# A fused sliding-window attention and MLP-mixer kernel: the last output block in three pieces, and all order lists searched anew

## The chip, the cores and the metric

The kernel runs on one core of a Trainium2 chip. The metric is the device time of one execution in microseconds (us); lower is better. Each version is run several times beside runs of the kernel before on the same chip. Every run here is fast, that is undisturbed; the clock that was granted to PE was 0.997 to 1.0 of full speed. A ratio is the mean time of one kernel's fast runs over that of the other's fast runs of the same rounds, so it isn't quite the ratio of the medians that are quoted beside it.

Besides the time there is one profiled execution of each kernel. Its span (from the first to the last instruction) is about 1.8 us shorter than the time, and positions inside it are read to 0.01 us.

## The reference, cut to what matters

```python
# attention: batch 8, heads 8, sequence 576, head size 64, window 128, ALiBi bias
scores = scale * q @ k.T + slopes * -(i - j)       # kept where 0 <= i - j < 128
attn = softmax(scores)
x = concat_heads(attn @ v)                         # (8, 576, 512)
# mixer
h = relu(x.T @ w_tok1) @ w_tok2                    # mixing over tokens, 576 -> 256 -> 576
u = x + h.T
out = u + relu(u @ w_ch1) @ w_ch2                  # mixing over channels, 512 -> 1536 -> 512
```

## The kernel before

Every piece of work has a short name, and five lists give the order in which the pieces are emitted; each engine then runs its own instructions in that order. A prime (') means the next batch. So while batch b is in the channel mixing, pieces of batches b+1 to b+3 are woven in.

- S: scores of a key block; A, AT: transposes of q and k on the tensor engine (PE), of strips and of the token tails; P, p: attention times v; K, k and U, u: the two steps of token mixing; UT: the second step for the last 64 tokens; X, x: transposes of u.
- C: a 128-wide strip of the first channel product (12 a batch, 4 matmuls of 512 columns each); D: an output block (12 such matmuls, in three parts D?0, D?1, D?2); T, E: the same for the token tails.
- q, l, qt, v, G, H: loads, of q, k, their tails, v, and the two channel weights. M: exponentials that make the mask. W: matmuls that only keep PE busy.

```python
def M():                         # three PSUM banks take turns, in the order of emission
    t = psM[mrot[0] % 3]
    mrot[0] += 1
    return t
...
def half(w):                     # only in the very last block, b == 7 and c == 3
    t = M()
    for ht in range(NHT):        # 12 matmuls of 256 columns
        nc.tensor.matmul(t[:, 0:256], lhsT=r2[b % 2][:, ht, c * P:(c + 1) * P],
                         rhs=WC2[:, ht, w:w + 256], start=(ht == 0), stop=(ht == NHT - 1))
    o = ob[orot[0] % len(ob)]
    orot[0] += 1
    nc.vector.tensor_tensor(out=o[:, 0:256], in0=t[:, 0:256], in1=ub[b % 2][:, c, w:w + 256], op=ALU.add)
    nc.sync.dma_start(out=out[b, c * P:(c + 1) * P, w:w + 256], in_=o[:, 0:256])
...
emit(PROLOGUE); emit(FIRST)      # batch 0 and the first scores of batch 1
emit(SECOND, 1)
for b in range(2, B - 1):
    emit(PERIOD, b)              # five times the same list
emit(LAST, B - 1)
```

A piece that asks for a bank may not start until the engine that empties that bank's last content has done so.

The softmax here doesn't subtract the row's maximum and nothing guards it: scores larger than these inputs give would overflow.

## Time and profile before

| | before |
|---|---|
| time, median | 288.33 us |
| span of the profiled execution | 286.7 us |
| PE busy | 278.9 us (97%) |
| VectorE, ScalarE, GpSimd busy | 57%, 41%, 35% |
| stops of PE of over 0.2 us after the first 11 us; the last is at 54 us | about 3.1 us |
| from the last matmul's end to the end of the span | 3.47 us |

A "stop" here is time by which a matmul starts later than its forerunner's length allows: 0.216 us after one of 512 columns, 0.109 after 256, 0.056 after 128. The profile's own idle time starts only where the earlier matmul's record ends, which is 0.16 us later, so it shows less, or nothing for a short stop. The chain of work that ended last, by engine, is nearly all PE:

```profile
PE 93%; ACT 3%; issue 1%; DVE 1%; DVEq 0%
```

### The profile page before, as it was taken

The numbers are of one execution on the slowest core, as the hardware profiler recorded it, in microseconds if no ns is written. First come the engines' busy times: TensorE is split into PE (matmuls) and PEld (weight loads), VectorE is DVE, ScalarE is ACT, GpSimd is POOL, SyncE is SP. The second block draws the span as 40 slices with busy tenths as digits, with TensorE's granted clock in tenths as the row PEclk, the third lists the DMA queues.
The fourth block names the chain that finished last, engine by engine and source line by source line (L and its number), as shares of the span: only waits on it lengthen the run. The fifth ranks groups of instructions, "written<-read, shape, count | busy, mean of one in ns | idle before, by whom it ended". The sixth has DMA issues, their size and how long they took to land.

```text
span 286.7 us, 6107 instructions
## 1 busy us (share of the span) xinstructions
PE 278.9 (97%) x2514; PEld 155.4 (54%) x2535; DVE 164.8 (57%) x329; ACT 118.6 (41%) x182; POOL 101.4 (35%) x132
## 2 busy tenths in 40 slices
PE   8999999999999999999999999999999999999995
PEld 3577546464565556545664456545664456455452
DVE  5359766537668376745556666745556666523222
ACT  3898941148515443326542343326542343104300
POOL 8997443099199029501870008900000000000000
PEclk9999999999999999999999999999999999999999
DMA  9999999799999989987999279999304310052032
GB/s 196 167 199 191 207 177 135 171 161 146 167 191 199 143 210 110 155 164 187 107 156 160 110 122 155 149 182 168 84 2 110 112 37 2 37 146 57 0 92 93
DMA packets 150267, 38.38 MB, mean 134 GB/s; under 512 B 137440, under 2 KB 145760, under 8 KB 150240
## 3 DMA queue, kind: packets, MB, share of 16 engines
q0 software_dynamic: 103152, 17.41, 84.0%
q1 hardware_dynamic: 46544, 20.06, 29.4%
q10 hardware_dynamic: 544, 0.52, 0.5%
q8 instruction: 20, 0.33, 0.5%
q14 instruction: 7, 0.06, 0.1%
HBM read 35.85 MB, written 9.44 MB: 158 GB/s over the span
## 4 chain that ended last, share of the span: by engine, by line
PE 93%; ACT 3%; issue 1%; DVE 1%; DVEq 0%
PE psM L548 29%; PE psM L607 28%; PE psM L506 4%; PE psM L481 4%; PE psS L356 4%; PE psT L565 4%; PE psM L629 4%; PE psS L420 2%; PE psS L416 2%; PE psT L750 2%; PE psS L448 1%; PE psM L588 1%; PE psS L360 1%; PE psM L234 1%; PE psM L490 1%
## 5 line engine op out<-in xcount | busy, mean ns | idle before, releaser
L548 PE MATMUL psM<-utb,WC 128*128 128x512 bf16 x384 | 90.9, 379 | 0.0
L607 PE MATMUL psM<-WC,r 128*128 128x512 bf16 x353 | 84.2, 379 | 0.7
L370 ACT ACTIVATE pe<-psS 128x1024 bf16<-128x1024 f32 x56 | 54.6, 1024 | 38.0 <-PE psS L356 34.4
L607 PEld LDWEIGHTS <-r 128*128 128x128 bf16 x372 | 34.5, 98 | 40.1 <-issue 3.1
L548 PEld LDWEIGHTS <-WC 128*128 128x128 bf16 x384 | 34.6, 98 | 36.3 <-issue 1.5
L376 DVE TENSOR_TENSOR pb<-pe,masks 128x1024 bf16<-128x1024 bf16 x42 | 29.0, 691 | 26.3 <-ACT pe L370 26.2
L554 ACT ACTIVATE r<-psM 128x512 bf16<-128x512 f32 x48 | 28.5, 599 | 35.5 <-PE psM L548 35.4
L190 POOL DMA_DIRECT2D qn<-in_q_dram x24 | 21.1, 907 | 59.2 <-DMA qT<-qn 58.7
L551 DVE TENSOR_SCALAR r<-psM 128x512 bf16<-128x512 f32 x48 | 32.6, 686 | 15.8 <-PE psM L548 15.6
L612 DVE TENSOR_TENSOR ob<-psM,ub 128x512 f32<-128x512 f32 x31 | 21.0, 687 | 27.4 <-PE psM L607 19.5
L190 POOL DMA_DIRECT2D vp<-in_v_dram x32 | 28.7, 928 | 0.7 <-PE psM L607 0.3
L190 POOL DMA_DIRECT2D kn<-in_k_dram x24 | 21.2, 911 | 18.1 <-DMA kT<-kn 11.8
L430 DVE TENSOR_TENSOR xb<-psS,rt 128x512 bf16<-128x512 f32 x28 | 19.4, 691 | 1.0
L508 DVE TENSOR_TENSOR ub<-psM,xb 128x512 bf16<-128x512 f32 x28 | 17.5, 681 | 2.6 <-PE psM L506 2.6
L568 ACT ACTIVATE r2t<-psT 128x512 bf16<-128x512 f32 x12 | 7.2, 600 | 24.8 <-PE psT L565 24.8
L420 PEld LDWEIGHTS <-pb 128*128 128x128 bf16 x224 | 13.5, 97 | 4.3 <-issue 1.0
L420 PE MATMUL psS<-vp,pb 128*128 128x65 bf16 x224 | 15.6, 193 | 0.0
L506 PE MATMUL psM<-r,W 128*128 128x512 bf16 x56 | 14.5, 379 | 0.5 <-DVE ob L612 0.5
L499 ACT ACTIVATE r<-psM 128x512 bf16<-128x512 f32 x7 | 4.2, 596 | 25.0 <-PE psM L490 25.0
L356 PE MATMUL psS<-qT,kT 64*128 64x256 bf16 x168 | 13.2, 271 | 0.7
L481 PE MATMUL psM<-xb,W 128*128 128x256 bf16 x112 | 13.4, 273 | 0.0
L565 PEld LDWEIGHTS <-WC 128*128 128x128 bf16 x192 | 11.6, 98 | 2.2
(134 smaller groups left out, 302.7 us busy)
## 6 DMA issues: line engine op xcount, KB each, us to landing
out_dram<-ob SPq DMA_DIRECT2D x31, 256.0 KB, 2.1
vp<-in_v_dram POOLq DMA_DIRECT2D x32, 128.0 KB, 5.4
kn<-in_k_dram POOLq DMA_DIRECT2D x24, 128.0 KB, 6.0
qn<-in_q_dram POOLq DMA_DIRECT2D x24, 128.0 KB, 6.1
WC<-in_moe_w_ch_dram POOLq DMA_DIRECT2D x3, 512.0 KB, 8.8
WC<-in_moe_w_ch_dram POOLq DMA_DIRECT2D x2, 768.0 KB, 14.2
out_dram<-ob SPq DMA_DIRECT2D x10, 128.0 KB, 2.3
qs<-in_q_dram POOLq DMA_DIRECT2D x3, 256.0 KB, 6.2
```

What stands on the lines that cost most here:

```text
L190: nc.gpsimd.dma_start(out=dst, in_=src[b, :, c * P:(c + 1) * P, :].rearrange("h s d -> s h d"))
L356: nc.tensor.matmul(s[h][:, a * 256:(a + 1) * 256], lhsT=kT[i][r, kb, hp, :], rhs=qT[i][r, kb:kb + 2, hp, :], start=True, stop=True)
L370: nc.scalar.activation(out=e[:, h, :], in_=s[n][:, None, :] if split else t2[:, :, :], func=ACT.Exp, scale=scale)
L376: nc.vector.tensor_tensor(out=p[:, :].rearrange("p (h x) -> p h x", h=2), in0=e[:, :, :], in1=masks[:, j].rearrange("p h g a x -> p h (g a ...
L420: nc.tensor.matmul(ov, lhsT=prob(b, qb, h, 0), rhs=vt[:, qb, h, 0:D + 1], start=first, stop=(hh == 3))
L481: nc.tensor.matmul(st["t"][h][:, dh * 256:(dh + 1) * 256], lhsT=W1[:, c, dh * P:(dh + 1) * P], rhs=by_half(xb[b % 2][:, c, :])[:, h], star ...
L506: nc.tensor.matmul(t[:, :], lhsT=W2[:, j, c * P:(c + 1) * P], rhs=r1[b % 2][:, j, :], start=(j == 0), stop=(j == 1))
L548: nc.tensor.matmul(t[:, :], lhsT=WC1[:, cb, ht * P:(ht + 1) * P], rhs=utb[b % 2][:, :, cb, :], start=(cb == 0), stop=(cb == NCB - 1))
L551: nc.vector.tensor_scalar(out=r2[b % 2][:, ht, :], in0=t[:, :], scalar1=0.0, scalar2=None, op0=ALU.max)
L554: nc.scalar.activation(out=r2[b % 2][:, ht, :], in_=t[:, :], func=ACT.Relu)
L565: nc.tensor.matmul(psT[:, j * P:(j + 1) * P], lhsT=WC1[:, cb, ht * P:(ht + 1) * P], rhs=utt[pi2][:, cb, :, :], start=(j == 0 and cb == 0), ...
L607: nc.tensor.matmul(t[:, :], lhsT=r2[b % 2][:, ht, c * P:(c + 1) * P], rhs=WC2[:, ht, :], start=(ht == 0), stop=(ht == NHT - 1))
```

## The change

The intent is to shorten the way from the last matmul to the end of the kernel (a smaller last addition and a smaller last store), and to search all order lists again, with the first loads of q named ahead of those of k.

```diff
-        def half(w):
+        def piece(w, n):
             t = M()
...
         if b == B - 1 and c == NC - 1:
-            return [lambda: half(0)] + [lambda: None] * (parts - 2) + [lambda: half(256)]
+            return [lambda: piece(0, 256), lambda: piece(256, P), lambda: piece(384, P)]
...
-U_ACT = (2,)
+U_ACT = (1, 2)          # strips of batch 0 whose residual PE adds, by identity matmuls
-X_DVE = (0, 2)          # which copies of X go to VectorE, the others to ScalarE
+X_DVE = (0, 3)
-K_DVE = (0,)            # which relu of K goes to VectorE
+K_DVE = (1,)
...
-SPLIT = (1, 2, 3, 4, 5) # scores of batch 0 whose exponential is done in two parts
+SPLIT = (0, 1, 2, 3, 4, 5)
...
-x_DVE = (0, 1, 2)       # as X_DVE and K_DVE, for the first batch
-k_DVE = (2, 3)
+x_DVE = (0, 2)
+k_DVE = (1,)
-AK_DVE = (1, 3, 6)      # which copies of transposes go to VectorE, which to ScalarE
-AQ_ACT = (0, 2, 4, 5, 6)
+AK_DVE = (3, 6, 7)
+AQ_ACT = (0, 1, 4, 5, 6, 7)
 PERIOD (its first third):
-Zq'' Lq''' C0 C7 T0 C6 C3 S31' S30' C4 P2' Zk'' Lk''' Y C10 C8 C9 P1' C2 T1 C1 P4' C11 P3' C5
+T1 C0 C6 C3 S30' S31' C2 Zq'' C7 C10 Zk'' T2 P2' C8 P3' C9 P1' C4 C5 T0 Lq''' C1 C11 P4' Y Lk'''
 LAST (its end):
-... D10 D30 D11 D20 D12 D31 D21 D22 D32
+... D10 D11 D12 D20 D21 D30 D22 D31 D32
 (PROLOGUE, FIRST and SECOND are all new too; cut)
```

More of the change, by code (lines that the diff above doesn't have):

```diff
@@ L19 @@
 U_DMA = (3, 4, 5, 6, 7)
-U_ACT = (2,)
-X_DVE = (0, 2)
-K_DVE = (0,)
+U_ACT = (1, 2)
+X_DVE = (0, 3)
+K_DVE = (1,)
 PROLOGUE = """
-l0 FC q0 J l1 O W4 q1 v4 q23 ck0 I l23 W3 W1 W2 B cq0 A0 ck1 v3 cq1 qt v0 s1 A1 S00 v2 t1 S20 W3
-ek v1 A3 A2 LW q01' AT l01' ex e2 S11 S30 l23' S21 M1 p0 LC S01 p1 k0 q23' e1 S31 u0 M0 M2 k1 G0
-p3 A1' qt' p2 A0' m0
+q0 q1 W3 J l0 l1 v4 FC l23 I ck0 W2 W4 W1 B v3 q23 cq0 O qt A0 ek ck1 s1 cq1 A1 S00 t1 v2 S20 W3
+v0 v1 LW A2 A3 AT q01' e2 S11 S30 l01' S21 ex M1 LC p0 l23' M2 p1 S01 k0 S31 u0 M0 m0 q23' G0 k1
@@ L27 @@
+p3 M3 A1' p2 qt' A0' v4'
 """
 FIRST = """
-A2' v3' G1 u1 k3 S10' A3' v4' G2 M3 H0 k2 H1 m1 v0' x0 AT' S00' v2' S20' u3 v1' W2 Lk'' UT u2
-Lq'' x3 Zq'' Zk'' x1 Lk''' x2 v0''' S30' E0 C5 v0'' S31' S01' v3'' C8 C9 C3 C11 C1 v1'' Lq'''
-S21' S11' C10 v2'' C7 C4 P4' C0 E2 C2 P0' C6 P3' v4'' v2''' D00 D01 P1' v4''' P2' D02 K0' K1'
-D10 D11 U1' D12 Zq''' X1' U3' U2' D20 U0' D21 D30 UT' Zk''' D22 S00'' D31 X0' D32 E1 T0' X2'
+G2 u1 G1 A3' S10' A2' k3 H1 AT' v2' e1 k2 v3' H0 x0 m1 v0' S00' S20' u3 W2 UT v1' Lq'' E0 Lk''
@@ L33 @@
+u2 x1 x3 Zq'' Zk'' Lk''' x2 v0'' S30' C2 C3 v0''' S01' S31' C11 C5 C1 Lq''' v1'' S21' v2'' S11'
+C0 C10 C7 v3'' C4 P4' v4''' E2 C8 P0' C9 v2''' C6 v4'' P3' P1' D00 P2' D01 D02 K0' K1' D10 D11
+U1' D12 U3' U2' X1' E1 D20 Zq''' Zk''' U0' D21 D30 D22 UT' S00'' D31 D32 X0' T0'
 """
 SECOND = """
-X3 Lq''' Lk''' S31' S30' T2 C10 v3''' S20' C5 S01' S11' v0''' C1 C8 C4 v1'' C11 C2 P0' C7 C9
-v3'' S10' S21' C3 C6 T1 C0 P2' v2''' v1''' P1' D00 D01 P3' P4' D02 K0' K1' S01'' S10'' D10 D11
-D12 v4''' U0' UT' U1' U3' U2' X0' S11'' S20'' D20 X3' D21 S00'' S21'' D22 E0 E1 X2' D30 E2 D31
@@ L38 @@
-X1' D32 P0''
+X2 X3 S30' S20' T1 Lq''' C1 C0 S11' Lk''' S01' T2 C5 v1'' S31' C3 P0' C10 C2 v3'' v3''' C4 S10'
+v0''' S21' C6 C11 C8 C7 v1''' v4''' C9 P2' P1' D00 P3' D01 D02 P4' K0' K1' S20'' S01'' D10 D11
+v2''' D12 U0' UT' U2' U3' X0' S11'' S10'' U1' D20 X3' D21 S21'' S00'' D22 E0 E1 X2' E2 D30 X1'
+D31 D32 P0''
 """
 PERIOD = """
-Zq'' Lq''' C0 C7 T0 C6 C3 S31' S30' C4 P2' Zk'' Lk''' Y C10 C8 C9 P1' C2 T1 C1 P4' C11 P3' C5
-K0' v4''' T2 K1' S01'' S00'' D00 v3''' v0''' D01 D02 U0' v1''' U3' UT' U2' U1' X1' P0'' v2'''
@@ L43 @@
-D20 D21 D10 X2' S10'' S11'' D11 X0' D22 D12 D30 D31 D32 S21'' S20'' X3' E0 E1 E2
+T1 C0 C6 C3 S30' S31' C2 Zq'' C7 C10 Zk'' T2 P2' C8 P3' C9 P1' C4 C5 T0 Lq''' C1 C11 P4' Y Lk'''
+K0' v0''' K1' S01'' v3''' S00'' v1''' D00 D01 D02 v2''' U1' v4''' U3' UT' U2' P0'' U0' D20 D21
+X2' X0' S10'' S11'' D10 D30 D11 D12 D22 D31 S20'' X1' S21'' D32 E0 E1 X3' E2
 """
 LAST = """
-T1 C0 C1 T0 Y C11 C2 C10 T2 C7 C3 C8 C6 C5 C4 C9 D00 E0 D01 D02 E1 E2 D10 D30 D11 D20 D12 D31
-D21 D22 D32
+C5 T0 Y C6 C0 C8 C10 C7 C1 C2 T1 C3 C11 T2 C9 C4 D00 E0 D01 D02 E1 E2 D10 D11 D12 D20 D21 D30
@@ L48 @@
+D22 D31 D32
 """
@@ L583, in ch2 @@
         st = {}
-        def half(w):
+        def piece(w, n):
             t = M()
             for ht in range(NHT):
-                nc.tensor.matmul(t[:, 0:256], lhsT=r2[b % 2][:, ht, c * P:(c + 1) * P],
-                                 rhs=WC2[:, ht, w:w + 256], start=(ht == 0), stop=(ht == NHT - 1))
+                nc.tensor.matmul(t[:, 0:n], lhsT=r2[b % 2][:, ht, c * P:(c + 1) * P],
+                                 rhs=WC2[:, ht, w:w + n], start=(ht == 0), stop=(ht == NHT - 1))
             o = ob[orot[0] % len(ob)]
             orot[0] += 1
-            nc.vector.tensor_tensor(out=o[:, 0:256], in0=t[:, 0:256], in1=ub[b % 2][:, c, w:w + 256],
+            nc.vector.tensor_tensor(out=o[:, 0:n], in0=t[:, 0:n], in1=ub[b % 2][:, c, w:w + n],
                                     op=ALU.add)
-            nc.sync.dma_start(out=out[b, c * P:(c + 1) * P, w:w + 256], in_=o[:, 0:256])
+            nc.sync.dma_start(out=out[b, c * P:(c + 1) * P, w:w + n], in_=o[:, 0:n])
         if b == B - 1 and c == NC - 1:
-            return [lambda: half(0)] + [lambda: None] * (parts - 2) + [lambda: half(256)]
+            return [lambda: piece(0, 256), lambda: piece(256, P), lambda: piece(384, P)]
         def part(pi):
```

## The prediction

> **What bounds the kernel now.** I read the page's first two parts first: which engine is full, and in which part of the span.
>
> ```profile
> PE 278.9 (97%) x2514; PEld 155.4 (54%) x2535; DVE 164.8 (57%) x329; ACT 118.6 (41%) x182; POOL 101.4 (35%) x132
> PE   8999999999999999999999999999999999999995
> PEclk9999999999999999999999999999999999999999
> ```
>
> PE is full in every slice but the first and the last, at full clock; no other engine passes 57%. Busy time alone can deceive, so I took the start-to-start times of neighbouring matmuls from the trace: a 512-column matmul follows its forerunner after 0.216 us through the whole channel-mixing work, so PE isn't only busy there but at its pace. The lines of the windows view divide the span into start, body and end:
>
> ```profile
> 0.00:14.00 14.00, 12.37 (x113) 5.87 (x113) 6.30 (x26) 8.22 (x15) 13.22 (x24) 1.00 1.46 181
> 14.00:34.00 20.00, 19.39 (x352) 14.62 (x351) 14.48 (x40) 17.74 (x38) 15.40 (x22) 1.00 1.43 198
> 130.00:260.00 130.00, 129.19 (x1101) 70.92 (x1111) 76.88 (x142) 48.57 (x68) 25.14 (x30) 1.00 0.87 112
> 281.70:286.70 5.00, 1.50 (x13) 1.07 (x11) 1.11 (x2) 0.00 (x0) 0.00 (x0) 1.00 0.36 131
> ```
>
> The reader is to see that 0.8 of 130 us is idle in the periodic body, that ACT is busy 17.74 of 20 us in the second stretch (the only place where another engine nearly binds), and that PE works only 1.5 of the last 5 us. What PE ever waited for, from the waits of PE alone, is short:
>
> ```profile
> PE psM L506 <- DVE ob L612: 0.5, 1, 0.5
> PE psM L234 <- DVE qT L239: 0.4, 1, 0.4
> PE psM L739 <- DVE ub L732: 0.2, 1, 0.2
> PE psM L259 <- DVE kT L239: 0.2, 1, 0.2
> ```
>
> Smaller stops hide in the 0.22 us that a matmul record lasts. Counting start-to-start excess, I find 0.53 and 0.35 us at 11.8 and 12.5 us (transposes of the first batch, waiting for a bank), 0.25 at 16.5 (scores S01, a bank), four of 0.24 from 23.0 to 27.1 (transposes of the second batch, waiting for ScalarE's copies), 0.39 at 30.1 and 0.63 at 53.6: 3.1 us in all, the whole stock from which an order alone can win. At the end, the timeline shows the path that sets the time:
>
> ```profile
> 281.73 1.47 PE L588 MATMUL psM<-WC,r 128*128 128x256 bf16 x12
> 281.93 0.69 DVE L612 TENSOR_TENSOR ob<-psM,ub 128x512 f32<-128x512 f32 x1 [1.03 <-PE psM L607]
> 283.24 0.42 DVE L592 TENSOR_TENSOR ob<-psM,ub 128x256 f32<-128x256 f32 x1 [0.62 <-PE psM L588]
> 283.69 0.33 SPq L594 DMA_DIRECT2D out_dram<-ob  x1
> ```
>
> The last matmul ends at 283.20; addition, store and landing (285.38 in the trace) follow one another, then 1.29 us of closing semaphores.
>
> **What the Trainium skill says.** "Perfetto Trace Analysis", section Identifying the Most-Contended Engine, warns that matmul busy share is no measure of nearness to the limit; here it agrees with the pace, since the pace is 0.216 us. "TensorE: Matmul & The Clock Gate", section Back-to-back issue gap, gives N/2.4 + 2.5 ns warm: 216, 109 and 56 ns for 512, 256 and 128 columns. The trace has 216, 109 and 56 to 57 (each with its own weight load), so the alternative of 81 ns for N=128 that the same section gives for a load-and-multiply stream isn't seen here. "VectorE: DVE Perf Modes", section on the TRN2 errata, gives (N+151)/0.96 ns for an fp32 tensor_tensor: 691, 424, 291; the rows have 687, 424 and 291 (the 128-column one from L690). "DMA: Bandwidth & Descriptors", section Anatomy of one DMA — SWDGE, has about 2.0 us of fixed cost; the last 128 KB store, on the other path, lands 1.70 us after its issue, so size hardly counts.
>
> **The change, part by part.**
> Final pieces. The last half of 256 columns becomes two of 128: 24 matmuls at 56 ns for 12 at 109. The last start moves from 281.73 + 11 x 0.109 = 282.93 to 281.73 + 23 x 0.056 = 283.01, and its record is 0.22 instead of 0.27 us long: end 283.23, 0.03 later. The addition shrinks from 0.424 to 0.291: the store starts at about 283.58 instead of 283.69. The earlier piece's addition is queued behind that of the 512-wide block, which ends at 282.62, so it is done by 282.95 and not in the way. Store: 64 instead of 128 KB, at most 0.1 quicker. Gain 0.1 to 0.2, say 0.12 us.
> U_ACT. The second strip of the first batch now adds its residual by four identity matmuls: 4 x 0.056 = 0.23 us more on PE, for certain; it frees 0.69 us of VectorE and puts 0.6 on ScalarE.
> Orders. A count of PE's instruction list shows only these 12 + 4 extra matmuls; changes between 64-row and 128-row work, at 0.09 us each, are 78 in both. So all else is about stops:
> - 11.1 to 13.6 us: the third strip's copies now go one to VectorE, one to ScalarE; before, both of the first pair stood in VectorE's queue. The two stops should fall from 0.87 to about 0.4, but VectorE then runs three copies of 0.69 from 11.60 to about 13.6, which the next scores need. They began at 13.69; gain 0.1.
> - 16.5: p1 now stands ahead of S01, so the bank has time: 0.25 gained. But M2 was moved up: four mask exponentials at 0.33 us instead of two ahead of S01's on ScalarE, which pushes the relu of k0 from 18.9 to about 19.2, ending 19.6, while u0, which needs it, would come at 19.3. Given back: net 0.
> - 23 to 27: A0' and A2' no longer stand side by side, u1 lies between. With ScalarE's copies at 0.48 us pitch, the three stops go; one of some 0.45 at AT', behind the 1.02 us exponential of S10', may stay. Gain 0.45.
> - 30.1: x1 stands before x3, whose copy was late; x2 still waits for the end of u2's copy. Gain 0.1.
> - 53.6: U3' stood one 0.23 us transpose after D12 and waited for D12's 0.69 us addition; now U3' takes a free bank for 0.43 us and U2' waits. Gain 0.2.
> - First v loads of batch 1: before, v0' landed at 40.89 and the first P0' began at 42.99. One more 128 KB load now stands ahead of it (pitch 0.87 us), so 41.8; P0' is placed about 1.1 us earlier, at 41.9. The slack is spent; I charge 0.15.
> - q ahead of k at the very start: q is issued by ACT and k by SP, at 0.73 and 0.74 us, in both kernels. No gain.
> - Body: loads and transposes keep their order on SP; on GpSimd only the v loads change places. 0.
>
> Sum: -0.12 + 0.23 - 0.1 - 0 - 0.45 - 0.1 - 0.2 + 0.15 = about -0.6. Discounted for steps that give back, -0.45 on 288.33: **287.9 us**.
>
> **The rivals.**
> 1. The stops are all removed. A search over the orders could reach what my block-by-block reading gives up: 3.1 us of stock less 0.23, plus 0.12 at the end, at best -3.0, in practice perhaps -1.5: 286.8. For it: the lists were changed everywhere. Against: the start is a chain of copies on ScalarE (17.74 of 20 us busy), which no order on PE shortens.
> 2. A new wait in the periodic body. It is repeated five times, so a stop of 0.3 us there costs 1.5: 289.8. For it: C blocks alternate between two evicting engines and new neighbours could put three on one; P3' and P1' stand nearer one another. Against: in the new order no more than three evictions of 0.69 stand on VectorE against 0.86 us of matmuls each, and K1' still has K0' (1.75 us) between it and P4'.
> 3. A late load: if v0' slips further than 0.9, P0' stops for it; another 0.5 would give 288.4.
> 4. The split is hidden: if the closing semaphores wait for some other store, the tail keeps its 3.5 us; 288.0.
>
> **Range and chances.** The three runs of before already spread by 0.6 us. Against that, my terms are each 0.1 to 0.5 and uncertain to half their size. 8 in 10: **286.9 to 288.7**. Faster by over 2% would need 5.8 us, nearly twice the stock of stops: 0.005. Slower by over 2% would need over 1 us in each period: 0.01. Within 2%: 0.985.
>
> **What would show it right or wrong.** PE busy should stay at 278 to 279.5 us and the spacing in the body at 0.216. Right: no stops at 23 to 24 us, the one near 53.6 down to about 0.4, a last 128-column addition of 0.29 us, its store issued about 0.35 us after the last matmul, and from that matmul's end to the span's end about 3.3 us instead of 3.47. Wrong: a PE wait on vp from a DMA near 42 us above 0.3 (rival 3), a wait on ScalarE or VectorE that returns every 32 us (rival 2), or first-batch relu waits near 19.3 above 0.5. If the first D block (44.59 before) starts before 43.9 with P1' now in front of it, the start won more than I give it (rival 1).

## The result, and the profile after

The changed kernel takes **287.95 us** (median of 5 runs, 287.49 to 288.23) against 288.33 us; the ratio is 0.9992, with a 95% interval of 0.9974 to 1.0009. By the times alone that is no difference. The two profiled spans are 286.67 and 286.18 us.

The page of the changed kernel, busy time of the engines, PE by slices, and the chain that ended last:

```profile
PE 277.5 (97%) x2532; PEld 155.8 (54%) x2551; DVE 165.4 (58%) x328; ACT 119.8 (42%) x185; POOL 101.5 (35%) x132
...
PE   8999999999999999999999999999999999999995
...
PE 83%; DMA 8%; POOL 6%; issue 1%; DVE 1%; POOLq 0%
```

PE looks as before. But the chain now runs through loads (DMA 8%) and GpSimd, which issues them, where it was PE from the start: at one point PE's progress has come to hang on a load. The windows view of the changed kernel, in the stretches shown of before (the last one is again the last 5 us; columns are the stretch, its length, then busy time and instructions of PE, weight loads, VectorE, ScalarE, GpSimd, then granted clock, DMA share and GB/s):

```profile
0.00:14.00 14.00, 12.29 (x121) 6.23 (x122) 7.32 (x29) 7.92 (x16) 13.16 (x25) 1.00 1.45 180
14.00:34.00 20.00, 19.27 (x354) 14.62 (x351) 13.29 (x35) 18.66 (x41) 14.62 (x20) 1.00 1.38 200
130.00:260.00 130.00, 128.83 (x1099) 70.61 (x1105) 77.76 (x142) 48.20 (x67) 25.16 (x30) 1.00 0.80 113
281.20:286.20 5.00, 1.72 (x26) 1.36 (x23) 1.25 (x3) 0.00 (x0) 0.00 (x0) 0.98 0.31 105
```

In the second stretch VectorE has 1.2 us less work and ScalarE 0.9 us more; it is now busy for 18.66 of 20 us. The waits of PE in the changed kernel (six of nine lines):

```profile
PE psM L607 <- issue: 1.8, 11, 0.2
PE psS L420 <- DMA vp<-in_v_dram: 0.5, 1, 0.5
PE psM L506 <- DVE ob L612: 0.3, 1, 0.3
PE psM L722 <- ACT r L713: 0.3, 1, 0.3
PE psM L259 <- ACT qT L239: 0.3, 1, 0.3
PE psM L234 <- DVE qT L239: 0.3, 1, 0.3
```

The first line is no wait: at these eleven places a matmul's record is missing. This also lowers the busy time of PE, 277.5 us; e1, whose PE does the same work and whose trace has all 2551 records, shows 279.2. Of the waits shown of before, those for VectorE's ub and kT have gone; three are new: for a load of v (L420, the block P0'), for a relu on ScalarE (L722, u0), and for a copy on ScalarE (L259, the tail transposes AT'). The end, from the timeline:

```profile
281.25 1.77 PE L588 MATMUL psM<-WC,r 128*128 128x128 bf16 x24
281.45 0.69 DVE L612 TENSOR_TENSOR ob<-psM,ub 128x512 f32<-128x512 f32 x1 [0.44 <-PE psM L607]
282.12 0.29 DVE L592 TENSOR_TENSOR ob<-psM,ub 128x128 f32<-128x128 f32 x1
282.60 1.12 SPq L594 DMA_DIRECT2D out_dram<-ob  x2
283.07 0.29 DVE L592 TENSOR_TENSOR ob<-psM,ub 128x128 f32<-128x128 f32 x1 [0.65 <-PE psM L588]
```

The 24 matmuls of the two small pieces take 1.77 us; at 56 ns each they should take 23 x 0.056 + 0.22 = 1.51. In the trace 0.275 us is lost between the first and the second matmul of the last piece, until 282.20, just after the 512-wide addition (281.45 + 0.69 = 282.14) is through.

Cutting both spans at the same places of the work gives a balance (positions in us from the span's start):

| stretch | before | after | difference |
|---|---|---|---|
| start, up to the scores S00 of the third batch (L356) | 59.48 | 59.57 | +0.09 |
| first channel-mixing matmul of batch 1's period to that of batch 7's | 61.77 to 257.01 = 195.24 | 61.86 to 256.54 = 194.68 | -0.56 |
| from there to the last matmul's start | 25.92 | 26.27 | +0.35 |
| last matmul's start to the end of the span | 3.75 | 3.37 | -0.37 |
| sum (spans: -0.49) | | | -0.49 |

So the start, where nearly all stops were, gained nothing; the body gained; and the two parts of the end nearly cancel.

### The profile page after: what moved, and what is told of

Its sections match the earlier page's. It is cut to its first block, busy times and chain, and to the rows that moved or that the text cites. A ratio compares the mean times of both kernels' runs of the same rounds, so it can differ in the third digit from the quotient of the medians.

```text
span 286.2 us, 6156 instructions
## 1 busy us (share of the span) xinstructions
PE 277.5 (97%) x2532; PEld 155.8 (54%) x2551; DVE 165.4 (58%) x328; ACT 119.8 (42%) x185; POOL 101.5 (35%) x132
## 3 DMA queue, kind: packets, MB, share of 16 engines
q1 hardware_dynamic: 46688, 20.06, 30.1%
## 4 chain that ended last, share of the span: by engine, by line
PE 83%; DMA 8%; POOL 6%; issue 1%; DVE 1%; POOLq 0%
PE psM L607 28%; PE psM L548 26%; DMA vp<-in_v_dram 5%; PE psM L481 4%; PE psM L506 4%; PE psT L565 4%; PE psM L629 4%; PE psS L356 3%; DMA WC<-in_moe_w_ch_dram 3%; PE psS L420 2%; PE psS L416 2%; POOL vp L190 2%; PE psS L448 1%; PE psM L490 1%; POOL qs L200 1%
## 5 line engine op out<-in xcount | busy, mean ns | idle before, releaser
L548 PE MATMUL psM<-utb,WC 128*128 128x512 bf16 x384 | 89.7, 379 | 0.0
L607 PE MATMUL psM<-WC,r 128*128 128x512 bf16 x353 | 83.3, 379 | 2.2 <-issue 1.8
L370 ACT ACTIVATE pe<-psS 128x1024 bf16<-128x1024 f32 x56 | 54.5, 1023 | 33.2 <-PE psS L356 30.1
L420 PE MATMUL psS<-vp,pb 128*128 128x65 bf16 x224 | 15.6, 193 | 0.5 <-DMA vp<-in_v_dram 0.5
L420 PEld LDWEIGHTS <-pb 128*128 128x128 bf16 x224 | 13.5, 97 | 4.4 <-DMA vp<-in_v_dram 1.0
L506 PE MATMUL psM<-r,W 128*128 128x512 bf16 x56 | 15.5, 379 | 0.3 <-DVE ob L612 0.3
L356 PE MATMUL psS<-qT,kT 64*128 64x256 bf16 x168 | 13.1, 271 | 0.0
```

The lines of the kernel that those rows point to most:

```text
L356: nc.tensor.matmul(s[h][:, a * 256:(a + 1) * 256], lhsT=kT[i][r, kb, hp, :], rhs=qT[i][r, kb:kb + 2, hp, :], start=True, stop=True)
L370: nc.scalar.activation(out=e[:, h, :], in_=s[n][:, None, :] if split else t2[:, :, :], func=ACT.Exp, scale=scale)
L420: nc.tensor.matmul(ov, lhsT=prob(b, qb, h, 0), rhs=vt[:, qb, h, 0:D + 1], start=first, stop=(hh == 3))
L506: nc.tensor.matmul(t[:, :], lhsT=W2[:, j, c * P:(c + 1) * P], rhs=r1[b % 2][:, j, :], start=(j == 0), stop=(j == 1))
L548: nc.tensor.matmul(t[:, :], lhsT=WC1[:, cb, ht * P:(ht + 1) * P], rhs=utb[b % 2][:, :, cb, :], start=(cb == 0), stop=(cb == NCB - 1))
L607: nc.tensor.matmul(t[:, :], lhsT=r2[b % 2][:, ht, c * P:(c + 1) * P], rhs=WC2[:, ht, :], start=(ht == 0), stop=(ht == NHT - 1))
```

## The experiments

"On" names the kernel that an experiment starts from. The ratio is to the kernel before, with its 95% interval.

| label | on | time, median | ratio | span |
|---|---|---|---|---|
| e1_v0_early | changed | 287.65 | 0.9975 (0.9960 to 0.9990) | 286.1 |
| e2_spare_bank | changed | 287.89 | 0.9984 (0.9966 to 1.0002) | 285.8 |
| e3_two_halves | changed | 287.74 | 0.9980 (0.9965 to 0.9995) | 285.7 |
| e4_masks_back | changed | 288.05 | 0.9993 (0.9976 to 1.0010) | 286.0 |
| e5_tail_load | changed | 288.02 | 0.9990 (0.9975 to 1.0005) | 286.5 |
| e6_both_loads | changed | 286.93 | 0.9960 (0.9943 to 0.9976) | 285.2 |
| e7_all_four | changed | 286.60 | 0.9945 (0.9930 to 0.9959) | 285.3 |
| e8_period_only | before | 287.69 | 0.9984 (0.9969 to 0.9999) | 285.9 |
| e9_q_first | e7 | 286.74 | 0.9942 (0.9927 to 0.9957) | 285.0 |
| e10_one_strip | e7 | 286.80 | 0.9945 (0.9929 to 0.9962) | 285.0 |
| e11_tail_between | e7 | 286.10 | 0.9922 (0.9907 to 0.9937) | 284.4 |
| e12_best | e7 | 286.09 | 0.9939 (0.9926 to 0.9951) | 284.3 |

All twelve gave the reference's result.

### e1_v0_early: one load of v earlier

```diff
 FIRST
-... H1 AT' v2' e1 k2 v3' H0 x0 m1 v0' S00' ...
+... H1 AT' v0' e1 k2 v3' H0 x0 m1 v2' S00' ...
```

> The changed kernel with two loads of the second batch exchanged (v0 ahead of the second half of the output weights, v2 behind it). Theory: the 0.64 us stop of PE before the first P0' near 41.6 us is the late landing of v0' (42.37 us) and nothing else; v0' now lands near 36.4, the stop falls to under 0.1, and everything after it starts 0.5 to 0.65 us earlier: span 285.6 instead of 286.2. Rival: the DMA queue is the limit at this place, so the wait moves to P3' or P1' (which read v2' and v1', landing near 42.4 and 43.2), and the span stays within 0.15 us of 286.2.

In the changed kernel the stop before P0' looks like this (timeline of PE, changed kernel):

```profile
40.92 1.02 PE L548 MATMUL psM<-utb,WC 128*128 128x512 bf16 x4
42.42 0.42 PE L420 MATMUL psS<-vp,pb 128*128 128x65 bf16 x8 [0.48 <-DMA vp<-in_v_dram]
```

With v0' moved, it landed at 36.96 instead of 42.37 us and this stop was gone. Yet the span was 286.13, as before the edit, so the theory's number failed. The rival's place (P3', P1') showed no stop either. The trace has the time elsewhere, and earlier: at the tail transposes (timeline of PE, e1):

```profile
25.46 0.22 PE L706 MATMUL psM<-xt,W1t 128*128 128x128 bf16 x1
26.90 0.38 PE L259 MATMUL psM<-ident,qkt 128*128 128x128 bf16 x4 [1.22 <-DMA qkt<-in_k_dram]
```

Here PE waits for another load, the q and k tails of batch 1. They landed at 26.76 us in this execution, and at 26.18 in the profiled one of the changed kernel, where the same place had cost 0.49 us. This made the next question: is it the loads as a whole that pace the start?

### e2_spare_bank: another bank for the last piece

```diff
         def piece(w, n):
-            t = M()
+            t = psT if w == 384 else M()
```

> The changed kernel with the very last 128-column piece in the PSUM bank that the tail work has left free. Theory: the 0.275 us stop inside the last piece (its first matmul against its second, 281.87 to 282.20 us) is the wait for the addition of the 512-wide block in the same rotating bank; with the free bank it is under 0.05, the last matmul starts 0.25 to 0.3 us earlier relative to the first matmul of that block, and the span shrinks by 0.15 to 0.3. Rival: VectorE's queue is the limit at the end (0.69 + 0.29 + 0.29 us of additions), so the last addition starts at the same place after the 512-wide block's end as now and the span keeps its length.

The theory held. From the first matmul after the periods (256.36) to the last matmul's start took 25.99 us instead of 26.27, 0.27 less. The span fell by 0.39 us, more than expected; 0.21 of this lies in the end (see e3), the rest in the start. End of e2, timeline:

```profile
281.07 0.83 PE L588 MATMUL psM<-WC,r 128*128 128x128 bf16 x12
281.27 0.69 DVE L612 TENSOR_TENSOR ob<-psM,ub 128x512 f32<-128x512 f32 x1 [0.44 <-PE psM L607]
281.74 0.83 PE L588 MATMUL psT<-WC,r 128*128 128x128 bf16 x12
```

The last piece now starts while VectorE still adds the 512-wide block. In the rotation of three, that block's bank is exactly the one that the last piece was given: block D2, piece D30, piece D31, and D32 is back at D2's bank.

### e3_two_halves: the pieces undone, the orders kept

```diff
-            return [lambda: piece(0, 256), lambda: piece(256, P), lambda: piece(384, P)]
+            return [lambda: piece(0, 256), lambda: None, lambda: piece(256, 256)]
```

> The changed kernel with the last block in two halves of 256 again, all orders as changed. Theory from the two traces: from the first matmul of the last half to the last matmul's start 1.20 us instead of 1.56 (with the 0.275 us stop), then 0.27 + 0.42 + 1.7 us to the landing instead of 0.22 + 0.29 + 1.6: the pieces are worth nearly nothing, this one is 0.0 to 0.15 us longer in span. Rival (the change's intent): the shorter last addition and store are a real gain, and this kernel is 0.3 us or more longer.

From the first matmul after the periods (256.08) to the end of the span it took 29.64 us; in the changed kernel 29.64, in e2 29.43. The three pieces as written are thus worth nothing, and 0.21 us once their bank is free. The span as a whole was 0.46 us shorter, where 0.0 to 0.15 longer was expected; all of that lies before the end, in the start. The times (287.74 against 287.95) are too coarse for this.

### e4_masks_back: mask exponentials behind u0 again

```diff
 PROLOGUE
-... p0 l23' M2 p1 S01 k0 S31 u0 M0 m0 ... p3 M3 A1' ...
+... p0 l23' p1 S01 k0 S31 u0 M0 m0 M2 ... p3 A1' ...
 FIRST
-... k3 H1 AT' v2' ...
+... k3 H1 AT' M3 v2' ...
```

> The changed kernel with the mask exponentials M2 behind M0 again (M3 pushed behind the tail transposes of the second batch). Theory: the 0.50 us stop of PE before u0 near 19.0 us is ScalarE's queue (four mask exponentials ahead of the exponentials of S01 and the relu of k0); with two of them there, that stop falls under 0.15 us. ScalarE still has the same sum of work up to 25 us, so part comes back at the transposes of the second batch: first channel-mixing matmul at 31.0 to 31.3 instead of 31.37. Rival: the start is bound by the sum of ScalarE's work, and the first channel-mixing matmul stays at 31.4 or later, the stop before u0 being replaced one for one by stops at 21 to 27 us.

The stop before u0 vanished: from the first matmul of k0 to that of u0 took 1.51 us instead of 1.91. But the first channel-mixing matmul came at 31.66 instead of 31.37, because PE again arrived earlier at the tail transposes and waited there 0.96 us for the loads. So the mechanism of the stop was as thought, the rival was right that nothing comes of it here, and its reason (ScalarE's sum of work) was wrong.

### e5_tail_load and e6_both_loads: what the loads allow

```diff
 PROLOGUE (both kernels)
-... M0 m0 q23' G0 k1 p3 M3 A1' p2 qt' A0' v4'
+... M0 m0 q23' qt' G0 k1 p3 M3 A1' p2 A0' v4'
 FIRST (e6 alone: v0' and v2' exchanged, as in e1)
```

> The changed kernel with the load of the second batch's q and k tails (two DMAs of 64 KB) ahead of the first third of the channel weights instead of behind it, nothing else. In the runs so far PE stopped at the tail transposes (L259 near 26 us) for 0.5 to 1.4 us, for a DMA in most of them, and that stop and the one before P0' near 41.6 us added up to 1.0 to 1.4 us in each run. Theory (the DMA queue paces the start): the tails land some 2 us earlier, the stop at L259 falls to 0.3 or less, PE arrives at P0' earlier by as much and now waits there for v0' (landing 42.2 to 42.5 us as before) 1.0 to 1.4 us; the span does not change by more than 0.15 us. Rival (each stop stands alone): the stop at P0' stays at 0.0 to 0.6 and the span falls by 0.5 to 1.0.

> Both loads of the second batch moved: the tails ahead of the first third of the channel weights and v0 ahead of the second half of the output weights. Theory: neither stop is left (L259 under 0.35, P0' under 0.1), the scores S00 of the third batch (L356 near 59.6) start 0.7 to 1.1 us earlier and the span falls to 285.0 to 285.5. Rival: the DMA queue gives a third stop (P3' or P1' for v2' and v1', or D00 for the output weights), and the span stays above 285.7.

In e5 the tails landed early enough (24.41 us), but the stop at L259 was still 0.51 us, now for ScalarE; 0.3 or less was expected. PE came to P0' only 0.08 us earlier than in the changed kernel; v0' landed 0.30 later (42.67 us), and PE waited longer (timeline of PE, e5):

```profile
40.84 1.02 PE L548 MATMUL psM<-utb,WC 128*128 128x512 bf16 x4
42.72 0.42 PE L420 MATMUL psS<-vp,pb 128*128 128x65 bf16 x8 [0.85 <-DMA vp<-in_v_dram]
```

By start-to-start times that is a stop of 1.02 us, up from 0.64, and the span (286.49) was 0.30 us longer than the changed kernel's, outside the 0.15 that was expected. With both loads moved, in e6, the same place has no stop at all:

```profile
40.54 1.02 PE L548 MATMUL psM<-utb,WC 128*128 128x512 bf16 x4
41.40 0.41 PE L420 MATMUL psS<-vp,pb 128*128 128x65 bf16 x8
```

The span fell to 285.18 us, as the theory had said, and the time to 286.93; the stop at L259 stayed at 0.49 us, for ScalarE, above the expected 0.35. Alone, neither load shows a gain in the span; together they are worth 1.0 us. In the start the queue of loads, which land one after another (128 KB every 0.85 us between 42 and 47 us), is a second clock. PE meets it in two places, and time won between two meetings is lost at the next.

The exchange itself is better seen in the changed kernel, e3, e4 and e2, whose loads stand in the same order, than in e5. From one to the next the stop at the tail transposes is longer, 0.49, 0.70, 0.96 and 1.10 us, and the stop before P0' is shorter or as short, 0.64, 0.33, 0.11 and 0.11. In these four and in e5, P0' starts 0.04 to 0.05 us after v0' has landed, be that at 41.91 us or at 42.67, and from the start of P0' to the end of the span it is always 243.8 us (243.6 in e2, which saves 0.2 in the end). So in these kernels, where v0' comes late, its landing alone sets the span.

### e7_all_four: the corrections together

```diff
 e6, with the free bank of e2 and the masks of e4
```

> The two loads moved, the last piece in a free bank, and the mask exponentials M2 and M3 back in ScalarE's queue. Theory: the savings add, since they are stops of PE at different places: 0.25 us at the last piece, 0.3 to 0.5 before u0, 0.7 to 1.1 by the loads; span 284.5 to 285.0, about 286.4 to 286.8 us on the clock of the runs, about 0.5% under the changed kernel. Rival: the masks come back as a stop at 26 to 31 us (they now stand ahead of the exponentials of the second batch), and the gain over the kernel with both loads moved is the bank's 0.25 alone.

The time was 286.60 us, below e6's 286.93. The profiled span, 285.27, missed the expected 285.0 (the other three runs had 284.6 to 285.0): PE stopped 0.65 us, until 11.30, for the first batch's q, which landed at 11.26 us in this execution. Apart from that the savings did add: from k0 to the first channel-mixing matmul 13.40 us against 13.78 in e6, so that putting the masks back is worth 0.38 us once the loads are out of the way, and the end was shorter by the bank's 0.2.

### e8_period_only: the periodic list alone, on the kernel before

```diff
-PERIOD of the kernel before
+PERIOD of the changed kernel
```

> The kernel before with the order list of the periods (batches 2 to 6) of the changed kernel alone. In the traces the changed kernel needed 0.06 to 0.09 us less in each period: between a 512-column matmul of the channel mixing and the first matmul of a P block the kernel before lost 0.08 us in each, the changed one nothing. Theory: the order alone does it: from the first channel-mixing block of batch 2's period to that of batch 7's 0.3 to 0.45 us less than in the kernel before (156.72 us from 100.29 to 257.01), the rest as before. Rival: it is the other lists or the engine assignments (the relu that went from ScalarE to VectorE), and this stretch stays within 0.1 us of 156.72.

The theory held. From batch 2's period to batch 7's it took 156.33 us (99.92 to 256.25); the changed kernel has 156.33, the kernel before 156.72. What the old list cost can be seen in any of its periods (timeline of the kernel before):

```profile
134.80 1.94 ACT L370 ACTIVATE pe<-psS 128x1024 bf16<-128x1024 f32 x2 [0.61 <-PE psS L365]
134.92 1.04 PE L548 MATMUL psM<-utb,WC 128*128 128x512 bf16 x4
135.87 0.19 PE L416 MATMUL psS<-vp,pb 128*128 128x65 bf16 x1
```

The first of the two exponentials ends at 135.82 and P2' uses the bank that it reads. Only one C block (0.86 us) stood between the scores and P2', and an exponential takes 1.02 us, so P2' started 0.08 us late, in each period. In the new list three C blocks stand there. Such a stop is shorter than the record of a matmul, and no list of waits shows it.

### e9_q_first, e10_one_strip, e11_tail_between: three more edits, each on e7

```diff
 e9, PROLOGUE
-... v4 FC l23 I ck0 W2 W4 W1 B v3 q23 cq0 ...
+... v4 FC q23 l23 I ck0 W2 W4 W1 B v3 cq0 ...
 e10
-U_ACT = (1, 2)
+U_ACT = (2,)
 e11, FIRST
-... D12 U3' U2' X1' E1 D20 ... D30 D22 UT' S00'' D31 ...
+... D12 U3' UT' U2' X1' E1 D20 ... D30 D22 S00'' D31 ...
```

> The kernel with all four corrections, and on GpSimd's queue the first batch's second half of q before that of k and of a v load, as the kernel before had it (the changed kernel has k, v, q). In four of the runs with the changed order q landed at 10.3 to 11.1 us and PE reached the transposes of the third strip at 11.0 to 11.4; where it landed late the wait shows as a DMA stop on qs of 0.2 to 0.5 us. Theory: q lands near 7.8 us, the DMA stop on qs is gone, the first scores S11 and all after it start 0.0 to 0.5 us earlier. Rival: k now lands last, at 9.6 to 10.5 us, and makes the same stop 0.25 us later in the same transposes; no gain.

In e9, q landed at 8.09 us and k at 9.42, and the stop was gone: from the first full scores block (L326) to p0 6.96 us, against 7.51 in e7. But 6.96 is also what the changed order needed when q happened to land by 10.6 us; the time (286.74) is no better than e7's. It takes away a risk, and is no gain in a usual execution.

> The kernel with all four corrections, and the second strip of the first batch again added on VectorE (U_ACT with 2 alone: four identity matmuls of 128 columns less, 0.6 us less on ScalarE, 0.69 us more on VectorE). Theory: PE has 4 x 0.056 = 0.22 us less to do, and ScalarE's chain up to the tail transposes (stop of 0.49 us at L259, which waits for a copy on ScalarE) is 0.5 us shorter, so the first channel-mixing matmul starts 0.2 to 0.6 us earlier. Rival: VectorE is late with the copies that follow in its queue (k of the two strips after it) and the stop moves to k3 or to the tail transposes with VectorE named; 0.0 or slower.

In e10 the rival was right that VectorE would be late, if not in the place: the stop came at the last q and k transposes of the second batch. PE had four matmuls less, but the addition went back to VectorE and PE waited for it:

```profile
PE psM L234 <- DVE ub L732: 0.5, 1, 0.5
```

From u0 to the first channel-mixing matmul it took 11.99 us, against 11.89 in e7. So in these traces the four identity matmuls cost PE 0.22 us and save 0.32: this part of the change is worth 0.10 us, too little for the times to show.

> The kernel with all four corrections, and the second batch's token-tail block UT (0.38 us of PE work in a bank of its own) moved from behind D22 to between U3 and U2, where PE stops 0.51 us for VectorE's addition of D12. Theory: the block fills the stop, which falls to 0.13 us, and the scores S00 of the third batch start 0.35 to 0.4 us earlier. Rival: VectorE is the limit of this stretch (D12, U3, U2, U0 additions of 0.69 us one behind another), and the stop reappears in front of U0 or D30; under 0.15 us.

The theory held. In the changed kernel U2' waits for a bank (timeline of PE, changed kernel):

```profile
53.65 0.59 PE L506 MATMUL psM<-r,W 128*128 128x512 bf16 x2
54.59 0.59 PE L506 MATMUL psM<-r,W 128*128 128x512 bf16 x2 [0.35 <-DVE ob L612]
```

In e11 the twelve small matmuls of UT', in a bank of their own, fill that gap, and U2' follows with a stop of 0.16 us by start-to-start times, which the profile doesn't show as idle (timeline of PE, e11; UT' left out):

```profile
52.45 0.59 PE L506 MATMUL psM<-r,W 128*128 128x512 bf16 x2
...
53.39 0.59 PE L506 MATMUL psM<-r,W 128*128 128x512 bf16 x2
```

The stretch from the first channel-mixing matmul to that of the next period took 29.50 us instead of 29.85, and the time was 286.10 us.

### e12_best

```diff
 e7, with the edits of e9 and e11
```

> All that held: both loads of the second batch moved, masks back, last piece in a free bank, UT between U3 and U2, and q ahead of k and of the v load in the first batch's half that GpSimd loads; the second strip stays with its identity matmuls, since taking them out gave nothing. Theory: the last two steps add 0.0 to 0.4 us (only in executions in which q would have landed after 10.5 us) to the kernel with UT moved: span 284.1 to 284.6, on the clock of the runs 285.7 to 286.2 us, 0.7 to 0.9% under the kernel before and 0.6 to 0.75% under the changed one. Rival: a further stop takes over, and it is no faster than 286.4.

The time was 286.09 us (6 runs, 285.99 to 286.96), and the span 284.32. Its stops of 0.3 us or more, by start-to-start times, lie in the first 12 us and at the tail transposes (0.31 us, until 25.63), and none comes later. It is 0.6% under the kernel before; 0.7 to 0.9% was expected. Against the changed kernel it is 1.86 us by the medians; the two were not run in the same rounds. By the times it is no faster than e11, whose ratio is even a little lower; these two are the fastest versions found.

## Why the prediction was right or wrong

The time, 287.95 us against 287.9 predicted, and the class (within 2%) were right. That the sum fits so well is luck. The prediction's terms give -0.47 us for the start, 0 for the body and -0.12 for the end; the spans show +0.09, -0.56 and -0.02. A start that won nothing and a body that won what the start was to win made up for one another.

**Right, with its size.**
- PE is the bound, at its pace, and only stops can be won: every gain and loss found is a stop added or taken away.
- The stop at AT' was predicted at 0.45 us behind an exponential on ScalarE; it was 0.49, and 0.49 to 0.51 in e5, e6 and e7, where the loads had no part in it. In the profiled changed kernel the tails landed so shortly before that this can't be separated, and in e1 to e4 the loads set it.
- p1 ahead of S01 was to win 0.25: p0 to k0 took 2.12 us instead of 2.38.
- The three stops from 23 us on went. The two stops at 11 to 13 us, 0.87 us together, were to fall to about 0.4: 0.47.
- The last addition was 0.29 us and its store was issued 0.36 us after the last matmul, as said.
- Changes between 64-row and 128-row work are equal in number, so they cost nothing.

**Right mechanism, wrong size.**
- The stop before u0 was put at 0.3 and taken as balanced by p1; it was 0.50, because S01's exponentials started at 18.01 us behind four masks. k0 to u0 lost 0.46 us; e4 showed the cause.
- U2' was to stop some 0.4 us for D12's addition, for a gain of 0.2. It stopped 0.51, where U3' had stopped 0.63 before: a gain of 0.11.
- v0': "The slack is spent; I charge 0.15". It landed at 42.37 instead of the assumed 41.8, since the 768 KB of weights now directly ahead of it landed later too (41.54), and P0' stopped 0.64 us. (In e2 to e4, with the same order of loads, v0' landed at 41.91 to 42.18.) This is rival 3, by the sign that the prediction had named for it, a wait for vp above 0.3 us. The step from the first channel-mixing matmul to the scores S00 of the third batch was to win 0.05 us and lost 0.38.

**Wrong.**
- "Body: ... 0." The body won 0.56 us. I had looked for new stops and counted the old body as free of them, because the list of waits showed none. Stops of 0.08 us in each of the five periods were there, between the exponential and P2'; e8 showed that the list alone takes them away, 0.39 us. The other 0.17 us lie in batch 1's period, where two more stops of 0.08 us (at 67.24 and 89.87 us in the kernel before) are gone; no experiment takes its list alone. So the 3.1 us were not "the whole stock".
- "0.8 of 130 us is idle in the periodic body" misread the view. All ten gaps that make up the 0.81 us are missing matmul records; in e1 and e8, whose traces have every record, PE is busy for 130.00 of these 130 us. For the same reason PE's busy time, 277.5 us, lies under the 278 to 279.5 that were named.
- At 30.1 us a gain of 0.1 was expected. One stop of 0.39 us became two, of 0.17 and 0.22 (until 30.25 and 30.70): no gain.
- "q ahead of k at the very start: ... No gain" looked at the first halves alone. The second half of q, now behind k and a load of v, landed at 10.33 us instead of 7.76, and where it came after 11.1 us PE stopped for it: 0.32 us in e4, 0.65 in e7. e9 undid this.
- The end was to win 0.12; it won 0.02 (29.66 us from the first matmul after the periods to the end of the span, now 29.64). The step "The earlier piece's addition is queued behind that of the 512-wide block ... and not in the way" looked at VectorE's queue only. What stood in the way was the bank: the third piece comes round to the 512-wide block's bank and loses 0.275 us. e2 showed this. Part of it came back, since the 64 KB store landed 1.59 us after its issue instead of 1.70; from the last matmul's end to the end of the span it took 3.15 us, where about 3.3 was named.
- The stop at AT' was seen as ScalarE's alone. In e1 to e4 it was a load's (AT' started 0.13 to 0.14 us after the tails had landed), up to 1.38 us, and the way in which one load's stop hides another's (e5, e6) was not in the prediction at all.

What stays open: I can't say how the first 31 us of the changed kernel and of the one before compare to better than 0.3 us, since the loads and PE's pace in the first 8 us differ from run to run by that much. The first transposes, which start in pairs, followed pair by pair after 0.106 us until 6.1 us in the profiled changed kernel, and after 0.053 from 5.45 us on in e2; the first full scores block started at 8.50 and 8.16 us. Nor can it be said what share each of the new lists and engine assignments has in the start, apart from those that e4, e9, e10 and e11 took alone.

## What to carry to other kernels

Where the bound engine is full, list its stops by start-to-start times rather than by idle time, since a stop shorter than the pipeline's depth shows nowhere else and may repeat in each period. Where an in-order queue of loads runs beside it, treat the queue as a second clock: work out at each meeting which of the two is late, and move all late loads together, because moving one only carries the wait to the next. When a piece of work is split, count through the rotation of buffers to see whose buffer the new last piece gets.

## What the Trainium skill lacked or had wrong

- "TensorE: Matmul & The Clock Gate", section Back-to-back issue gap, gives about 81 ns per matmul for a stream of weight loads and matmuls of 128 columns, and about 131 for 512 columns. Here each of 12 pairs of 128 columns takes 56 ns (e2: 0.83 us for 12, of which 0.22 is the last one's record), and the channel mixing, with a weight load for each matmul of 512 columns, goes at 216 ns. The prediction used the section's other formula, for single matmuls, which fits both.
- "TensorEngine Tiling (Array Packing)" says that changing the tiling mode drains the engine, but gives no time. Here a change between 64-row and 128-row matmuls costs 0.09 to 0.10 us where nothing else delays it; the traces have 82 of them in either kernel (the prediction counted 78).
- "DMA: Bandwidth & Descriptors", section Anatomy of one DMA — SWDGE, has 2.0 us plus bytes over 436 GB/s for one DMA. For a load queued behind others that says little: 128 KB of v took 14.9 us from issue to landing in the changed kernel, and what counts is its place in the queue and the 0.85 us pitch.
